# Attention beside a 2-D Fourier filter on one core: the order of the memory terms, and the place of the transposition of the maxima

## The chip, the core and the metric

The kernel runs on one core of one Trainium2 chip. Its time is the device time of one execution in microseconds, as the median of the runs. The engines are named as in the profile: PE (TensorE, with PEld for its weight loads), DVE (VectorE), ACT (ScalarE), POOL (GpSimd) and SP (SyncE, which here only issues transfers).

## What is computed

Two independent heads share one output. The second, a Fourier transform of a 2048 x 576 array, a multiplication and the way back, is not touched by the change. The first is attention with a compressive memory, with 32 heads of 18 columns, over 2048 rows in 4 segments of 512:

```python
for s in range(N):                                  # 4 segments, in order
    logits = einsum("bhqd,bhkd->bhqk", qs, ks) * scale + mask
    a_dot  = einsum("bhqk,bhkd->bhqd", softmax(logits), vs)
    pq  = phi(qs)                                   # phi(t) = t+1 if t>0 else exp(t)
    num = einsum("bhld,bhde->bhle", pq, M)
    den = einsum("bhld,bhd->bhl", pq, z)[..., None] + 1e-6
    outs.append(g * (num / den) + (1 - g) * a_dot)  # g = sigmoid(beta), per head
    M = M + einsum("bhld,bhle->bhde", phi(ks), vs)
    z = z + einsum("bhld->bhd", phi(ks))
```

The rows of all segments are then multiplied by `wo`.

## The kernel before

**Stages.** The program is written out in full by Python, each engine gets its instructions in the order in which the code emits them, and semaphores are set where one engine's instruction needs another's. The forward transform, the projections and the inverse transform fill the time until about 360 us; `ATT.attention` (line 894) does the rest.

**Steps.** `attention` runs 133 steps `t`. A step handles one head of one segment, so 32 steps make a segment, and four steps make a group `k` with its heads `hh` = 0 to 3 ("first" to "fourth" head; the third head's step is `hh==2`). Two groups share a stack `n` of queries `Qs` and keys `Ks` that SP loads from DRAM in six pieces of 144 KB each (`stack_dmas`, line 611). Three pipelines are ten steps apart:

- `s1(t+10)` (629): scores of a head ten steps ahead, for their maxima only. TensorE makes three products into PSUM tiles `s1` (three buffers) and VectorE reduces each (L646, and L640 twice), 512, 512 and 256 columns.
- `mpath` (654), once a group: in the second head's step VectorE, ScalarE and POOL gather the 16 maxima of each row and split them into two bf16 parts `mh` (L658 to L662). TensorE transposes `mh` into a tile `mt` (L665), which takes one of the three `s1` buffers. ScalarE copies it to `mts` (L668, one buffer), and POOL issues a transfer of 8 KB that puts it into two rows of `Qs` (L669). The group needs it when its own steps begin, so that the second product subtracts the maximum.
- `s2(t)` (671): scores with the maximum subtracted, in three products (L679, L683 and L684, L688) into three buffers `s2`, and ScalarE's exponentials into `P`. In the fourth head's step the half above the diagonal is set to zero for the whole group by four instructions, on POOL (L692) for groups 0 to 28, on VectorE (L694, a minimum with a table `cap`) for groups 29 and 30.
- `pv` (700): `P` times the values, five steps later.

**Work in the background.** A list `bg` of generators is advanced by `run_bg` (906): one piece in the middle of a step, and a second at the end of every fifth step (the rate is 1.2). When a segment's outputs of the softmax part are in DRAM (`uD`), a lane fetches the row sums, takes reciprocals and loads tiles `ux` (line 788, three buffers; SP issues), and then appends three jobs to `bg`:

- `combine(g-1)` (792), nine pieces, for the five tiles of 126 rows of segment `g-1`. Piece by piece: TensorE spreads the reciprocals into `pb` (L808), VectorE multiplies `ux` by it (L813), POOL adds the memory term `am` (L814); two pieces later ScalarE rounds the sum to `oh` (L803) and POOL takes the remainder `ol` (L804). From step 117 on VectorE does POOL's two. The loads of `ux` tiles 3 and 4 are issued one step after the pieces of tiles 0 and 1, whose buffers they take.
- five `mem1(g,u)` (775), two pieces each, the memory terms of segment `g` for later use: TensorE's product `pn` (L778), ScalarE's copy to `am` (L780), a load of the next segment's `pq` one step later; then `pb` (L784) and VectorE's multiply (L785).
- `den(g+1)` and `oproj(g-1)`, the denominators and the product with `wo` (L829).

All of these products use one PSUM buffer, tag `post`, so each waits until the engine that reads the one before has finished. The jobs run for `g` = 1, 2, 3, from about steps 51, 84 and 115; below these are the first, second and third time.

## Time and profile before

| | us |
|---|---|
| median of 3 runs shown | 738.96 |
| the three runs | 740.35, 734.36, 738.96 |
| the profiled execution, its own time | 736.84 |
| its span on the core | 735.1 |
| TensorE busy in the span | 691.1 |
| VectorE busy | 553.4 |
| ScalarE busy | 457.9 |
| POOL busy | 204.2 |

A row of a timeline gives start and length in us, engine, line, operation, what it writes and reads, and shape; brackets hold the engine's idle time before it and what ended it. Several of a kind in a row are merged (x4). A row of busy time by stretch gives the stretch, its length, and for each engine the busy time and the number of instructions, then the granted clock of TensorE as a share of full speed, the share of time in which the DMA engines were busy, and GB/s. TensorE's products overlap, so a busy TensorE is not TensorE at its peak, and an idle gap is a lower bound of what was lost.

### The profile page before, as it was taken

The numbers are of one execution on the slowest core, as the hardware profiler recorded it, in microseconds if no ns is written. First come the engines' busy times: TensorE is split into PE (matmuls) and PEld (weight loads), VectorE is DVE, ScalarE is ACT, GpSimd is POOL, SyncE is SP. The second block draws the span as 40 slices with busy tenths as digits, with TensorE's granted clock in tenths as the row PEclk, the third lists the DMA queues.
The fourth block names the chain that finished last, engine by engine and source line by source line (L and its number), as shares of the span: only waits on it lengthen the run. The fifth ranks groups of instructions, "written<-read, shape, count | busy, mean of one in ns | idle before, by whom it ended". The sixth has DMA issues, their size and how long they took to land.

```text
span 735.1 us, 14249 instructions
## 1 busy us (share of the span) xinstructions
PE 691.1 (94%) x4879; PEld 496.6 (68%) x4879; DVE 553.4 (75%) x1285; ACT 457.9 (62%) x1012; POOL 204.2 (28%) x405
## 2 busy tenths in 40 slices
PE   4998999999999999999999999999999899998897
PEld 4988779879779788899744444443665345653396
DVE  6999879899799788787688878876567575668333
ACT  3666796585585664444487777776566566568521
POOL 2111000100200112565065335462334832325100
PEclk9999999999999999999999999999999899999999
DMA  9884435655373468899547656777456565431231
GB/s 337 264 267 148 144 116 180 197 173 160 133 236 113 169 206 277 213 219 219 179 99 185 168 149 162 179 177 145 117 142 161 142 156 131 108 115 41 70 123 64
DMA packets 83243, 121.04 MB, mean 165 GB/s; under 512 B 11352, under 2 KB 50630, under 8 KB 83036
## 3 DMA queue, kind: packets, MB, share of 16 engines
q1 hardware_dynamic: 76580, 104.11, 49.9%
q0 software_dynamic: 6592, 16.03, 8.0%
q8 instruction: 38, 0.62, 0.3%
q14 instruction: 33, 0.27, 0.1%
HBM read 81.78 MB, written 38.24 MB: 163 GB/s over the span
## 4 chain that ended last, share of the span: by engine, by line
PE 70%; DMA 13%; DVE 7%; ACT 5%; issue 3%; POOL 1%; SPq 1%; ACTq 0%; DVEq 0%; POOLq 0%
PE pj L459 14%; PE pv L709 8%; PE po L829 7%; PE pjv L459 7%; PE s L636 4%; PE i L307 4%; PE i L296 3%; PE s L644 3%; PE s L679 3%; DMA x<-qkD 2%; DMA Ks<-qkD 2%; DMA Qs<-qkD 2%; PE pn L778 2%; PE po L858 2%; PE s L683 2%
## 5 line engine op out<-in xcount | busy, mean ns | idle before, releaser
L640 DVE CUSTOM_DVE_ANT_0 junk<-s,mask 128x512 bf16<-128x512 f32 (+1 forms) x256 | 141.2, 551 | 62.6 <-PE s L636 59.0
L646 DVE TENSOR_REDUCE mx<-s 128x4 f32<-128x512 f32 x128 | 87.9, 687 | 12.0 <-PE s L645 9.2
L692 POOL TENSOR_SCALAR_AFFINE_SELECT P<-P 128x512 f32<-128x512 f32 x116 | 70.0, 634 | 73.9 <-ACT P L680 66.0
L709 PE MATMUL pv<-P,vs 128*32 128x512 f32 (+3 forms) x1024 | 89.3, 445 | 0.3 <-DVE P L694 0.3
L680 ACT ACTIVATE P<-s 128x512 f32<-128x512 f32 x128 | 76.3, 596 | 17.4 <-PE s L679 15.0
L689 ACT ACTIVATE P<-s 128x256 f32<-128x256 f32 x128 | 49.1, 384 | 50.9 <-PE s L688 50.9
L685 ACT ACTIVATE P<-s 128x512 f32<-128x512 f32 x128 | 76.0, 594 | 0.3 <-PE s L684 0.3
L459 PE MATMUL pj<-x,wqkh 128*128 128x512 f32 x162 | 56.5, 409 | 0.0
L206 DVE TENSOR_TENSOR Z<-t,t 128x290 f32<-128x290 f32 (+1 forms) x96 | 48.4, 553 | 0.1
L206 DVE TENSOR_TENSOR t<-Z 128x580 f32<-128x580 f32 x64 | 46.0, 754 | 0.0
L506 POOL MEMSET vt<- 128x32 f32 x16 | 2.3, 161 | 153.8 <-PE pm L516 128.7
L636 PE MATMUL s<-Ks,Qs 108*128 108x512 bf16 (+1 forms) x128 | 42.2, 330 | 0.1
L142 PE MATMUL f<-ftab,eh 128*128 128x290 f32 (+1 forms) x160 | 31.4, 315 | 10.1 <-DMA ftab<-ftab 10.1
L296 PE MATMUL i<-civ,Y 128*128 128x256 f32 (+1 forms) x288 | 38.5, 285 | 1.5 <-POOL Y L281 0.9
L296 PEld LDWEIGHTS i<-civ,Y 128*128 128x128 f32 (+1 forms) x288 | 35.9, 181 | 2.3 <-POOL Y L281 1.3
L709 PEld LDWEIGHTS pv<-P,vs 128*32 128x32 f32 x1024 | 22.4, 109 | 21.9 <-issue 14.6
L645 PE MATMUL s<-tri,idb 128*128 128x256 bf16 x128 | 35.2, 275 | 1.3 <-ACT idb L585 1.3
L307 PE MATMUL i<-itab,T 128*128 128x290 f32 (+1 forms) x224 | 36.0, 309 | 0.0
L459 PE MATMUL pj<-xh,wqkl 128*128 128x512 f32 x90 | 35.5, 395 | 0.0
L459 PE MATMUL pj<-x,wqkl 128*128 128x512 f32 x90 | 35.5, 395 | 0.0
L459 PE MATMUL pj<-xh,wqkh 128*128 128x512 f32 x90 | 35.5, 395 | 0.0
L459 PEld LDWEIGHTS pj<-x,wqkh 128*128 128x128 f32 x162 | 30.4, 188 | 7.2 <-issue 0.6
(211 smaller groups left out, 1830.5 us busy)
## 6 DMA issues: line engine op xcount, KB each, us to landing
qkD<-sp SPq DMA_DIRECT2D x36, 384.0 KB
Ks<-qkD SPq DMA_DIRECT2D x72, 144.0 KB
x<-qkD SPq DMA_DIRECT2D x60, 144.0 KB
Qs<-qkD SPq DMA_DIRECT2D x60, 144.0 KB
xin<-xb SPq DMA_DIRECT2D x16, 384.0 KB
cfw<-cfw POOLq DMA_DIRECT2D x16, 384.0 KB, 4.9
civ<-civ POOLq DMA_DIRECT2D x16, 384.0 KB, 7.6
vs<-vD SPq DMA_DIRECT2D x16, 330.0 KB
```

What stands on the lines that cost most here:

```text
L206: v.tensor_tensor(o,a,b,op=op)
L296: nc.tensor.matmul(p[:m,k],Y[i][:,q,c*128:c*128+m],cc[:,hl,o:o+256],start=n==0,stop=n==5)
L307: nc.tensor.matmul(p,x,t,start=n==0,stop=n==6)
L459: s.nc.tensor.matmul(out,a,b,start=i==0,stop=i==len(L)-1)
L636: nc.tensor.matmul(out,Q[:108,h,128*i:128*i+128],K[:108,h,:128*(i+1)],start=True,stop=True)
L640: nc.vector.tensor_tensor_reduce(out=junk[:,:w],in0=src,in1=s.mask[:,512-w:],scale=1.0,scalar=-3.0e38, op0=OP.add,op1=OP.max,accum_out=s.m ...
L646: nc.vector.tensor_reduce(out=s.mx[k][:,hh],in_=pa.rearrange("p (b c) -> p b c",c=128),axis=mybir.AxisListType.X,op=OP.max)
L680: nc.scalar.activation(P[0][:,hh],p0,AF.Exp,scale=SC)
L685: nc.scalar.activation(P[1][:,hh],p1,AF.Exp,scale=SC)
L692: if k<29: nc.gpsimd.affine_select(out=x,in_=x,pattern=pat+[[1,128]],compare_op=OP.is_ge,fill=0.0,base=0,channel_multiplier=-1)
L709: nc.tensor.matmul(s.pvt[32*hh:32*hh+32,128*j:],vt[:,j,19*h:19*h+32],mv[0][:,hh,mv[1]],start=j==0,stop=j==2,skip_group_check=True)
L829: nc.tensor.matmul(ps,a[t][:r,c],b[:r,t,w],start=i==0,stop=i==14)
```

## The change

A new generator `mixed` takes the place of `combine` and the five `mem1` in `bg`. It has the same 19 pieces in another order: five pieces of `combine` first, then memory pieces (`m`) and pieces of `combine` (`c`) in turn. `mpath`'s transposition, which stood in the fourth head's step ahead of the last product of `s2`, moves to the end of the third head's step, and the copy and the transfer's issue move to the beginning of the fourth head's step.

```diff
+    def mixed(s,g):
+        c=s.combine(g-1); M=[s.mem1(g,u) for u in range(5)]
+        for x in "cccccm"+"cmmcmmcmmcmm"+"m":
+            if x=="c": next(c,None); yield
+            else:
+                while M:
+                    try: next(M[0]); break
+                    except StopIteration: M.pop(0)
+                yield
+        for _ in c: pass
+        for m in M:
+            for _ in m: yield
...
-                    bg.append(s.combine(g-1))
-                    for u in range(5 if g<4 else 0): bg.append(s.mem1(g,u))
+                    bg.append(s.mixed(g))
...
             if qu: qu.pop(0)()
+            if hh==3 and m is not None: steps(m,1)
             steps(a,1)
...
             steps(a,1)
-            if hh==3 and m is not None: steps(m,1)
             steps(b,1)
-            if hh==3 and m is not None: steps(m,1)
+            if hh==2 and m is not None: steps(m,1)
```

POOL's queue at a group early in attention (group 2; `P_4719` to `P_4721` are its exponentials, `wol` a piece of the late set-up):

```order
+L669 DMA Qs_3320<-mts 2x16x128
 L608 TENSOR_TENSOR wol<-ob,woh 126x576
 L692 AFFINE_SELECT P_4719<-P_4719 128x4x128
 L692 AFFINE_SELECT P_4720<-P_4720 128x4x128 x2
 L692 AFFINE_SELECT P_4721<-P_4721 128x4x128
-L669 DMA Qs_3320<-mts 2x16x128
```

The issue of the transfer of the maxima now stands ahead of the group's four zero settings, and here of a piece of the set-up too.

VectorE's queue the second time, at steps 86 and 87 (`L813` multiplies tile 3 of `ux`, the `L640` and `L646` rows are reductions of `s1` scores):

```order
+L640 ISA junk,mg<-s_7797,mask 128x256
+L640 ISA mg 128x1
+L646 TENSOR_REDUCE mx<-s_7811 128x4
+L640 ISA junk,mg<-s_7819,mask 128x512
+L640 ISA mg 128x1
 L813 TENSOR_TENSOR ux<-ux,pb 126x512
-L640 ISA junk,mg<-s_7801,mask 128x256
```

The multiply of tile 3 stands one step's reductions later than before; a memory product has taken its place in step 86.

VectorE's queue the third time, at steps 119 and 120 (the first two rows are the multiply and the sum of tile 3, the `L694` rows the four minima of group 29, `L785` the multiply of memory tile 0, and the rows behind it the work on tile 4):

```order
 L813 TENSOR_TENSOR ux<-ux,pb 126x512
 L814 TENSOR_TENSOR am<-ux,am 126x512
+L694 TENSOR_TENSOR P_9064<-P_9064,cap 128x4x128
+L694 TENSOR_TENSOR P_9065<-P_9065,cap 128x4x128 x2
+L694 TENSOR_TENSOR P_9066<-P_9066,cap 128x4x128
+L785 TENSOR_TENSOR am<-am,pb 126x512
 L804 TENSOR_TENSOR ol<-am,oh 126x512
 L813 TENSOR_TENSOR ux<-ux,pb 72x512
 L814 TENSOR_TENSOR am<-ux,am 72x512
```

The minima now stand right behind tile 3 and ahead of the first memory multiply. TensorE's queue in the changed step 120, from its second product of `s2` on (`pb` and `pn` both go into the `post` buffer):

```order
L684 MATMUL s_9196<-x_2763,Ks_3323 128x128
L784 LDWEIGHTS sel
L784 MATMUL pb<-rd,sel 126x512
L688 LDWEIGHTS Ks_3323
L688 MATMUL s_9203<-x_2763,Ks_3323 128x256
L778 MATMUL pn<-pq,Mst_64 126x512
```

Memory tile 0's second product and memory tile 1's first now stand in one step; before, step 120 had neither.

## The prediction

> **What bounds the kernel now.** I read the page's engine table first, then its clock row, then busy time by stretch, and last every pause of TensorE in time order, each with its releaser.

> ```profile
> span 735.1 us, 14249 instructions
> PE 691.1 (94%) x4879; PEld 496.6 (68%) x4879; DVE 553.4 (75%) x1285; ACT 457.9 (62%) x1012; POOL 204.2 (28%) x405
> ...
> PEclk9999999999999999999999999999999899999999
> ```

> TensorE is busy for 94% of the span and the clock is full but for one slice. The change touches the attention stage alone, from about 360 us. There TensorE's program is the path and its pauses are what can be won. Where the clock falls is seen by stretch:

> ```profile
> 573.00:579.60 6.60, 3.46 (x31) 1.65 (x30) 3.24 (x10) 4.18 (x10) 5.00 (x5) 0.98 0.76 198
> 579.60:586.20 6.60, 6.50 (x25) 2.39 (x25) 4.12 (x14) 2.88 (x7) 6.56 (x9) 0.50 0.48 108
> 668.00:692.50 24.50, 20.05 (x146) 7.48 (x142) 14.55 (x25) 18.52 (x43) 4.93 (x8) 1.00 0.23 71
> ```

> The columns are length, busy time of PE, PEld, DVE, ACT and POOL, granted clock, DMA share, GB/s. In the first stretch TensorE stood for 6.60 − 3.46 = 3.14 us, and in the next it ran at half clock: 6.50 × 0.5 = 3.25 us lost. The third is the end of attention's steps, with 24.50 − 20.05 = 4.45 us of idle.

> The pauses that the change can touch are these (start, length, instruction, and in brackets the idle time before it and what ended it):

> ```profile
> 384.87 0.39 PE L679 MATMUL s<-Qs,Ks 110*128 110x512 bf16 x1 [0.43 <-DMA Qs<-mts]
> ...
> 394.44 0.39 PE L679 MATMUL s<-Qs,Ks 110*128 110x512 bf16 x1 [1.49 <-DMA Qs<-mts]
> ...
> 406.47 0.38 PE L644 MATMUL s<-x,Qs 108*128 108x384 bf16 x2 [0.52 <-DMA Ks<-qkD]
> ...
> 453.72 0.38 PE L644 MATMUL s<-Ks,x 108*128 108x384 bf16 x2 [0.27 <-DVE mg L640]
> 455.70 0.38 PE L644 MATMUL s<-Ks,x 108*128 108x384 bf16 x2 [0.61 <-DVE mx L646]
> ...
> 476.52 0.38 PE L644 MATMUL s<-x,Qs 108*128 108x384 bf16 x2 [1.22 <-DMA Ks<-qkD]
> ...
> 481.92 0.38 PE L644 MATMUL s<-x,Qs 108*128 108x384 bf16 x2 [0.28 <-DVE mg L640]
> 483.76 0.38 PE L644 MATMUL s<-x,Qs 108*128 108x384 bf16 x2 [0.22 <-DVE mx L646]
> ...
> 495.02 1.12 PE L778 MATMUL pn<-pq,Mst 126*126 126x512 f32 x2 [0.89 <-DVE am L785]
> ...
> 569.86 0.38 PE L808 MATMUL pb<-rr,sel 96*126 96x512 bf16 x1 [0.55 <-DVE ux L813]
> ...
> 575.47 0.38 PE L808 MATMUL pb<-rr,sel 96*72 96x512 bf16 x1 [1.10 <-DVE ux L813]
> 576.42 0.22 PE L665 MATMUL mt<-idb,mh 128*128 128x128 bf16 x1 [0.33 <-DVE mx L646]
> 577.03 0.38 PE L644 MATMUL s<-x 108*128 108x384 bf16 x2 [0.28 <-DVE mg L640]
> 579.68 0.37 PE L636 MATMUL s<-x 108*128 108x256 bf16 x1 [1.51 <-DVE mg L640]
> ...
> 589.07 0.38 PE L784 MATMUL pb<-rd,sel 96*126 96x512 bf16 x1 [0.51 <-ACT am L780]
> ...
> 603.44 0.38 PE L784 MATMUL pb<-rd,sel 96*126 96x512 bf16 x1 [0.45 <-ACT am L780]
> ```

> **Part 1: the transfer of the maxima.** POOL issues it today behind the four zero settings, and TensorE's first product of the next group but one needs it:

> ```profile
> 385.61 2.40 POOL L692 TENSOR_SCALAR_AFFINE_SELECT P<-P 128x512 f32<-128x512 f32 x4
> 387.95 0.61 POOL L669 DMA_DIRECT2D Qs<-mts  x1
> ...
> DMA to landing us min/median/max: 2.0/5.0/7.6
> ...
> 384.90 0.25 ACT L668 COPY mts<-mt 32x128 bf16<-32x128 bf16 x1 [0.37 <-DMA Qs<-mts]
> ```

> In the changed order the transposition comes one step (about 2.1 us) sooner and the issue no longer waits 2.40 us for the zeros, so the issue moves up by about 3 us. The two waits on it, 0.43 + 1.49 = 1.92 us, are then covered. But right behind them TensorE waits for loads of the stacks (0.52 us at 406.47), and SyncE issues those at the pace at which earlier loads land:

> ```profile
> 394.00:406.00 12.00, 11.51 (x92) 5.18 (x92) 9.30 (x29) 9.17 (x23) 4.39 (x9) 1.00 0.74 188
> ```

> At a DMA share of 0.74 these loads move up only in part. The bounds are 0 (all of it is waited for again at 406) and −1.92; ScalarE's copy of the maxima (0.37 us of wait, with the copy that SyncE's next store needs behind it) goes earlier too, so I take the middle, −1.0. The selects start one transfer's issue (0.61 us) later; their first reader comes two steps on, so that is nothing, and without this cover 0.61 us a group.

> **Part 2: the transposition in the third head's step.** It now waits for POOL's split of the maxima with one step less between. At the regular pace it fits, and its PSUM tile shifts the rotation of three `s1` tiles. So far the fourth head's tile shortened the lead over VectorE at the start of the next group; that is where 453.72 to 455.70 (0.27 + 0.61, behind a reciprocal) waited. Now it is shortened one step sooner, where the second score product of the step waits for the last reduction of the step before:

> ```profile
> 424.67 0.28 PE L636 MATMUL s<-Ks,Qs 108*128 108x256 bf16 x1
> ...
> 425.46 0.38 PE L636 MATMUL s<-Ks,Qs 108*128 108x512 bf16 x1
> ...
> 424.99 0.42 DVE L640 CUSTOM_DVE_ANT_0 junk<-s,mask 128x256 bf16<-128x256 f32 x1 [0.29 <-PE s L636]
> 425.34 0.08 DVE L640 DVE_READ_ACCUMULATOR2_ANT mg<- 128x1 f32 x1
> ```

> The reduction is over at 425.42 and TensorE comes at 425.46, or 0.06 us later with the transposition ahead of it: it just fits. Price 0, gain −0.8 (bounds 0 and −0.88). TensorE's earlier arrival at 476.52, where loads are waited for again, gives back some of parts 1 and 2: 0 to +1.8, taken as +0.5.

> **Part 3: memory terms between the tiles, first time (steps 51 to 65).** The pauses at 481.92, 483.76 and 495.02 go: 0.28 + 0.22 + 0.89 = −1.4. New: step 55 holds a combination tile and a memory multiply, with one `post` bank between them, priced by the like pause at 569.86, 0.55, and step 58 a multiply ahead of the tight reduction, 0.4. Sum −0.5, bounds −1.4 and +0.5. With the memory steps the loads of the next third's `pq` move too: on SyncE's queue one passes ahead of four stack pieces here and one ahead of two in part 4. Among TensorE's pauses none waits for a stack from 484 to 604 us, so this costs 0; uncovered it would be one load's place in that queue.

> **Part 4: the second time (steps 84 to 97).** Here VectorE multiplied tiles 3 and 4 before they had been loaded:

> ```profile
> 574.73 0.69 DVE L813 TENSOR_TENSOR ux<-ux,pb 126x512 f32<-126x512 f32 x1 [2.56 <-DMA ux<-uD]
> ...
> 578.60 0.68 DVE L813 TENSOR_TENSOR ux<-ux,pb 72x512 f32<-72x512 f32 x1 [1.63 <-DMA ux<-uD]
> ...
> 568.95 0.32 SPq L791 DMA_DIRECT2D ux<-uD  x1
> ```

> The load of tile 3 landed about 5.7 us after its issue (568.95 to 574.7), and nothing moves it. The multiply of tile 3 moves one step on, past a product `pn` of 1.1 us, to about 575.0, against 574.7 for the landing; that of tile 4 moves four steps on. So 1.10 + 0.33 + 0.28 + 1.51 goes, and with it the drop of the clock, 3.25; 0.51 and 0.45 go as well, and one pause of 0.5 is new in step 90. Sum: −6.9, bounds −7.4 and 0 (rival 3).

> **Part 5: the third time (steps 115 to 127).** Here the change costs. From step 117 on VectorE does this work instead of POOL, and the zeros of the last groups too:

> ```profile
> 670.31 0.68 DVE L813 TENSOR_TENSOR ux<-ux,pb 126x512 f32<-126x512 f32 x1
> 671.02 0.69 DVE L814 TENSOR_TENSOR am<-ux,am 126x512 f32<-126x512 f32 x1
> ...
> 673.55 2.49 DVE L694 TENSOR_TENSOR P<-P,cap 128x512 f32<-128x512 f32 x4
> ...
> 669.77 0.66 POOL L661 CAST mh<-mg 128x16 bf16<-128x16 f32 x1
> 670.52 0.22 POOL L662 TENSOR_TENSOR mh<-mg,mh 128x16 bf16<-128x16 f32 x1
> ...
> 671.04 0.38 PE L808 MATMUL pb<-rr,sel 96*72 96x512 bf16 x1 [0.96 <-DVE ux L813]
> ```

> In before's clock: the transposition of the last maxima, now in step 118, waits for POOL, 670.74 less the 0.61 of the transfer that has gone ahead: to 670.1, a pause of 0.7. ScalarE then finishes two exponentials and the cast at about 672.3; VectorE does subtraction, multiply and sum of tile 3 until 674.2, the four minima (2.49) until 676.7, and only then the multiply of memory tile 0, until 677.4. Step 120's two products both need the one `post` bank: `pb` waits for the first multiply (1.25 us, to 673.65), `pn` for the last (673.9 to 677.4, 3.45 us). Later ones of 0.5 and 0.7 make 6.6 us of pauses against 4.45: +2.1; followed step by step I get +0.9, since ScalarE has caught up meanwhile. I take +1.5, bounds 0 and +2.1. With 4.7 us of standing in 5.05 us, denser than the 3.14 of 6.60 at 573 us, I expect the clock to drop here as it did there: +3.25, bounds 0 and 3.25.

> [...]

> **Sum**: −1.0 − 0.8 + 0.5 − 0.5 − 6.9 + 1.5 + 3.25 = −3.95 us. The profiled execution took 736.84 us (span 735.1 and 1.7 around it), which gives 732.9; it lies 2.1 us under the median of the runs shown, 738.96, and the runs spread over 6 us. Against the median: 735.0.

> **Rivals.** (1) The clock holds at step 120, because the pause is shorter or cut up differently: −3.95 − 3.25 = −7.2, 731.8 us. For it speaks that ScalarE and VectorE may run ahead; against it that the pause is longer than the one that did drop it. (2) Slower: the tight reduction of part 2 does not fit. A pause of s in each of 31 groups costs 31 s; it decides from s = 0.13 us, and at 0.4 us it is +12.4 − 3.95 = +8.4, 747.4 us. Against it: the margin is measured, if 0.04 us, and the same margin held at the place that the change frees. (3) The load of tile 3 lands later than 575, VectorE's queue stands at step 87 and the clock drops there as before: part 4 is nothing, +2.95, 741.9 us. For it: the margin is 0.3 us. Against it: tile 4, the longer pause, has margin. (4) The change doesn't speed up the transfers' stage, since the stacks' loads bind: parts 1 and 2 nothing, 736.3 us; within the forecast's range.

> **How the numbers follow.** Chances: forecast (with 4) 0.52, rival 1 0.22, rival 2 0.10, rival 3 0.12, others 0.04. Likeliest 735.0 us, alone 731.5 to 738.5. The range 729.5 to 742.0 takes in rival 1 with the runs' spread and rival 3, and leaves out rival 2 and little else. 1% is 7.4 us, about what a measurement of this kernel tells from no change: faster than 731.6 takes rival 1 at its better half and a tail of the forecast, 0.2; slower than 746.4 is rival 2 and a tail of rival 3, 0.11; within, 0.69.

> **What would show it.** Right: no wait on `mts` in TensorE's rows; the granted clock 1.00 through 570 to 590; no VectorE wait on `ux` in part 4; a pause before `pn` (L778) in step 120 of about 3.4 us with VectorE's minima ahead of its multiply, and half clock for some 6 us behind it. Wrong: pauses of TensorE's score product L636 behind VectorE's reductions in every third and fourth head (rival 2), or a wait on `ux` at step 87 (rival 3). A longer wait at 406 or 476 would show parts 1 and 2 given back.

## The result and the profile after

The changed kernel takes 734.62 us (median of 17 runs, 730.96 to 738.64), the kernel before 736.53 us in as many runs beside it (734.25 to 740.35). The ratio, with its 95% interval in brackets, is 0.9962 [0.9946, 0.9977] (the two medians alone give 0.9974): 0.4% faster, 1.7 to 4.0 us, on the quick side of "within 1%". The forecast of 735.0 us is met to 0.4 us, partly by luck: it set −3.95 us against a median of three runs, 738.96, that lies 2.4 us above the median of 17.

The profiled execution took 735.37 us. The first lines of its page:

```profile
span 733.7 us, 14245 instructions
...
PE 691.2 (94%) x4879; PEld 497.7 (68%) x4879; DVE 552.7 (75%) x1285; ACT 457.4 (62%) x1012; POOL 204.6 (28%) x405
...
PEclk9999999999999999999999999999999999998999
```

The slice with the low clock has moved: it lay at 580 us before, it lies at 670 us now. The busy times are nearly those of before, so what changed is waits and the clock. The starts of a step's product at L679 show where the time went. For the last steps, first before, then after (the first row is the start of step 118, the last that of step 127):

```profile
667.01 0.38 PE L679 MATMUL s<-Qs,Ks 110*128 110x512 bf16 x1
...
688.81 0.38 PE L679 MATMUL s<-x,Ks 110*128 110x512 bf16 x1
```

```profile
660.52 0.38 PE L679 MATMUL s<-Qs,Ks 110*128 110x512 bf16 x1
...
687.02 0.38 PE L679 MATMUL s<-x,Ks 110*128 110x512 bf16 x1
```

These steps took 21.80 us and take 26.50: +4.70. The same subtraction for each stretch of steps, of this kernel and of those of the experiments below, in us against before:

| kernel | 0 to 51 | 51 to 65 | 84 to 97 | 118 to 127 |
|---|---|---|---|---|
| the change | −0.03 | −2.30 | −6.61 | +4.70 |
| transposition and transfer alone | +0.70 | −1.03 | −1.36 | +0.85 |
| mixture alone | −1.17 | −1.35 | −6.59 | +4.83 |
| third time in the old order | +1.16 | −2.45 | −6.61 | +0.85 |
| filler in step 120 | −2.60 | −1.54 | −6.58 | +3.10 |
| group 29's zeros on POOL | +0.42 | −2.49 | −6.61 | +4.19 |
| loads of `pq` early | −3.58 | −1.35 | −6.61 | +4.25 |
| third time old, `pq` early | −3.70 | −2.63 | −6.60 | +2.44 |
| mixture in the first two times alone | −0.73 | −1.50 | −6.60 | +2.69 |
| before, `pq` early | +0.81 | +1.44 | −0.85 | +0.01 |
| without group 29's zeros | −2.31 | −2.76 | −6.59 | +1.86 |

What lies between the columns moves by 0.8 us at most. Of the change itself the columns sum to −4.2 us; it started attention 2.42 us later than before did (363.04 against 360.62), with the same program up to there. Part of that, 1.7 us at most (half of its length, an estimate), is a clock drop of 3.4 us at 292.64, at a granted clock of 0.50 and ahead of attention: the six profiled executions with such a drop (the change and numbers 1, 2, 5, 6 and 9) start attention 1.57 to 3.22 us later than before's, the five others from 1.26 us sooner to 0.99 later. So much differs from one execution to the next, and a column is to be believed where several kernels repeat it: that for 84 to 97 does (−6.58 to −6.61 in nine kernels). The first does not as a whole; the account of part 1 below takes it apart.

TensorE's pauses after (start, length, instruction; in brackets the idle time before it and what ended it), those that answer to the rows of the prediction:

```profile
408.27 0.38 PE L644 MATMUL s<-x,Qs 108*128 108x384 bf16 x2 [1.79 <-DMA Ks<-qkD]
...
458.11 0.38 PE L644 MATMUL s<-Ks,x 108*128 108x384 bf16 x2 [1.03 <-DVE mx L646]
...
478.13 0.38 PE L644 MATMUL s<-x,Qs 108*128 108x384 bf16 x2 [0.75 <-DMA Ks<-qkD]
484.31 0.38 PE L784 MATMUL pb<-rd,sel 96*126 96x512 bf16 x1 [0.56 <-DVE am L811]
...
578.89 1.07 PE L709 MATMUL pv<-P,vs 128*32 128x512 f32 x8 [0.38 <-POOL P L692]
584.12 0.38 PE L784 MATMUL pb<-rd,sel 96*126 96x512 bf16 x1 [0.49 <-DVE ux L813]
...
663.42 0.23 PE L665 MATMUL mt<-idb,mh 128*128 128x128 bf16 x1 [0.36 <-POOL mh L662]
666.96 0.38 PE L784 MATMUL pb<-rd,sel 96*126 96x512 bf16 x1 [1.18 <-DVE ux L813]
670.69 2.07 PE L778 MATMUL pn<-pq,Mst 126*126 126x512 f32 x2 [3.24 <-DVE am L785]
680.64 0.27 PE L688 MATMUL s<-x,Ks 110*128 110x256 bf16 x1 [0.42 <-ACT P L689]
681.62 0.38 PE L679 MATMUL s<-x,Ks 110*128 110x512 bf16 x1 [0.71 <-ACT P L680]
684.63 1.12 PE L778 MATMUL pn<-pq,Mst 126*126 126x512 f32 x2 [0.67 <-DVE am L785]
689.72 1.08 PE L778 MATMUL pn<-pq,Mst 72*72 72x512 f32 x2 [0.67 <-DVE am L785]
```

Four things are to be seen. No row between 380 and 400 us waits on `mts` any more, but the wait for the stacks has grown from 0.52 to 1.79 us (below it is the wait at step 21: it stands between the starts of steps 21 and 22 at L679, and the product that waits is the first of step 22). The pauses around 576 us (1.10, 0.33, 0.28, 1.51) are gone. Step 55 has its new pause of 0.56. And step 120 holds 1.18 and 3.24 us. The clock, by stretch:

```profile
405.28:408.69 3.41, 1.62 (x14) 0.49 (x7) 1.51 (x6) 1.17 (x4) 0.41 (x2) 1.00 0.66 171
408.69:412.11 3.42, 3.42 (x17) 1.05 (x16) 1.72 (x4) 1.31 (x3) 0.00 (x0) 0.50 0.64 142
...
564.00:580.00 16.00, 14.94 (x122) 6.93 (x120) 13.91 (x39) 11.80 (x27) 13.21 (x18) 1.00 0.72 186
...
664.69:668.10 3.41, 1.58 (x11) 0.67 (x7) 2.45 (x4) 2.94 (x7) 0.26 (x1) 1.00 0.03 5
668.10:674.90 6.80, 4.21 (x13) 1.16 (x13) 2.53 (x5) 2.08 (x4) 0.00 (x0) 0.50 0.01 2
```

It holds where it dropped before (564 to 580 and on), and within attention it drops behind the two places where pauses are dense: for 3.4 us at 408.69 and for 6.8 us at 668.10.

VectorE's rows at step 120 show what `pn` waits for:

```profile
665.62 0.69 DVE L804 TENSOR_TENSOR ol<-am,oh 126x512 fp32r<-126x512 f32 x1 [3.99 <-ACT oh L803]
666.23 0.68 DVE L813 TENSOR_TENSOR ux<-ux,pb 126x512 f32<-126x512 f32 x1
666.94 0.69 DVE L814 TENSOR_TENSOR am<-ux,am 126x512 f32<-126x512 f32 x1
667.55 2.49 DVE L694 TENSOR_TENSOR P<-P,cap 128x512 f32<-128x512 f32 x4
669.95 0.68 DVE L785 TENSOR_TENSOR am<-am,pb 126x512 f32<-126x512 f32 x1
```

The first row waits 3.99 us for ScalarE's cast, and VectorE's queue behind it goes row by row: multiply and sum of tile 3, four minima, and only then the multiply of memory tile 0 that frees the bank.

### The profile page after: what moved, and what is told of

Read it like the earlier page. It is cut to its first block, busy times and chain, and to the rows that moved or that the text cites. A ratio compares the mean times of both kernels' runs of the same rounds, so it can differ in the third digit from the quotient of the medians.

```text
span 733.7 us, 14245 instructions
## 1 busy us (share of the span) xinstructions
PE 691.2 (94%) x4879; PEld 497.7 (68%) x4879; DVE 552.7 (75%) x1285; ACT 457.4 (62%) x1012; POOL 204.6 (28%) x405
## 4 chain that ended last, share of the span: by engine, by line
PE 70%; DMA 12%; DVE 8%; ACT 5%; issue 3%; POOL 2%; SPq 0%; DVEq 0%; ACTq 0%; POOLq 0%
PE pj L459 14%; PE pv L709 9%; PE po L842 7%; PE pjv L459 7%; PE s L636 4%; PE s L644 3%; PE s L679 3%; DMA yb<-yout 3%; PE i L307 2%; PE i L296 2%; PE pn L778 2%; PE s L683 2%; PE po L871 2%; DMA x<-qkD 2%; PE f L142 2%
## 5 line engine op out<-in xcount | busy, mean ns | idle before, releaser
L640 DVE CUSTOM_DVE_ANT_0 junk<-s,mask 128x512 bf16<-128x512 f32 (+1 forms) x256 | 141.2, 551 | 60.0 <-PE s L636 53.9
L646 DVE TENSOR_REDUCE mx<-s 128x4 f32<-128x512 f32 x128 | 87.9, 687 | 11.5 <-PE s L645 8.7
L680 ACT ACTIVATE P<-s 128x512 f32<-128x512 f32 x128 | 77.4, 605 | 15.6 <-PE s L679 11.9
L685 ACT ACTIVATE P<-s 128x512 f32<-128x512 f32 x128 | 77.3, 604 | 0.3 <-PE s L684 0.3
L692 POOL TENSOR_SCALAR_AFFINE_SELECT P<-P 128x512 f32<-128x512 f32 x116 | 69.8, 637 | 6.0 <-ACT P L689 3.2
L636 PE MATMUL s<-Ks,Qs 108*128 108x512 bf16 (+1 forms) x128 | 42.2, 330 | 0.0
```

Of the source, the lines that this page charges most:

```text
L636: nc.tensor.matmul(out,Q[:108,h,128*i:128*i+128],K[:108,h,:128*(i+1)],start=True,stop=True)
L640: nc.vector.tensor_tensor_reduce(out=junk[:,:w],in0=src,in1=s.mask[:,512-w:],scale=1.0,scalar=-3.0e38, op0=OP.add,op1=OP.max,accum_out=s.m ...
L646: nc.vector.tensor_reduce(out=s.mx[k][:,hh],in_=pa.rearrange("p (b c) -> p b c",c=128),axis=mybir.AxisListType.X,op=OP.max)
L680: nc.scalar.activation(P[0][:,hh],p0,AF.Exp,scale=SC)
L685: nc.scalar.activation(P[1][:,hh],p1,AF.Exp,scale=SC)
L692: if k<29: nc.gpsimd.affine_select(out=x,in_=x,pattern=pat+[[1,128]],compare_op=OP.is_ge,fill=0.0,base=0,channel_multiplier=-1)
```

## The experiments

Theory: the gain is the second time's order (pauses and a clock drop gone), the third time's order gives most of it back through VectorE's queue and a clock drop, and the earlier transfers gain nothing since the stacks' loads bind behind them. The rivals stand in each expectation. All ratios are to the kernel before.

**1. The transposition and the transfer alone.** In the loop of before, `combine` and `mem1` stay:

```diff
+            if hh==3 and m is not None: steps(m,1)
             steps(a,1)
...
-            if hh==3 and m is not None: steps(m,1)
             steps(b,1)
-            if hh==3 and m is not None: steps(m,1)
+            if hh==2 and m is not None: steps(m,1)
```

> Before, with the moves of the maxima alone (transposition in the third head's step, transfer ahead of the zeros); the memory terms stay in their old order. The forecast's terms for these two parts sum to -1.0 - 0.8 + 0.5 = -1.3 us against before. From the changed kernel's trace, where the wait for loads of the stacks behind these parts grew from 0.52 to 1.79 us and the waits at the start of the following group stayed, I now expect about 0 (-0.6 to +0.6 by the steps up to 47), and +1.7 more if the clock drops behind the longer wait. The pauses of 1.10, 0.28 and 1.51 us at steps 86 to 90 and the clock drop behind them must be there as in before. Rival: the transfers were the bound of that stretch and the gain is -1.9 us or more, with no longer wait at step 21.

Measured: 0.9983 [0.9956, 1.001], and +0.70 us in the steps to 51. The wait behind the transfers grew further:

```profile
408.14 0.41 PE L644 MATMUL s<-x,Qs 108*128 108x384 bf16 x2 [2.65 <-DMA Ks<-qkD]
...
579.63 0.37 PE L636 MATMUL s<-x 108*128 108x256 bf16 x1 [1.39 <-DVE mg L640]
```

The clock dropped behind the first (408.4 to 411.8) and, as in before, at 579.0 to 585.8; of the 1.10 us before tile 4's product 0.31 stayed. The +0.70 us lies 0.4 us below the least that was expected with a drop. The rival falls, and the second time's gain isn't this part's, but for 1.4 us of its pauses.

**2. The mixture alone**: the change with the three `mpath` lines at their old places.

> The changed kernel with the transposition and the transfer back at their old places: the mixture alone. By the theory that the whole effect is the mixture's, the attention steps end about 3.9 us earlier than in before: -2.3 in the first time (steps 51 to 65), -6.6 in the second (84 to 97), +5.0 in the third (115 to 127); the waits on the transfers of the maxima (0.43 and 1.49 us) and the reciprocal's pauses stand as in before, and the wait for the stacks at step 21 is about 0.5. Rival: the gain at steps 84 to 97 needs the earlier transposition too (the pause behind the reduction of the maxima, 1.51 us, would stay); then -6.6 shrinks to about -3 and the whole is about 0.

Measured: 0.9963 [0.9941, 0.9984], the ratio of the whole change, and columns −1.35, −6.59, +4.83. Of the waits on the maxima 0.25 and 1.47 us stand, and none for the stacks at step 21:

```profile
386.42 0.39 PE L679 MATMUL s<-Qs,Ks 110*128 110x512 bf16 x1 [0.25 <-DMA Qs<-mts]
395.97 0.39 PE L679 MATMUL s<-Qs,Ks 110*128 110x512 bf16 x1 [1.47 <-DMA Qs<-mts]
...
669.67 2.07 PE L778 MATMUL pn<-pq,Mst 126*126 126x512 f32 x2 [3.25 <-DVE am L785]
```

By the medians the mixture is the whole effect; the rival, that the second time needs the transposition too, falls. In the first time the mixture alone is 0.95 us short of the change, but the seven kernels with both range from −1.35 to −2.76, and the load's wait in that stretch from none to 1.51 us, so that a share of the transposition there isn't shown.

**3. The third time in the old order.**

```diff
-                    bg.append(s.mixed(g))
+                    if g<3: bg.append(s.mixed(g))
+                    else:
+                        bg.append(s.combine(g-1))
+                        for u in range(5): bg.append(s.mem1(g,u))
```

> The changed kernel with the third time (steps 115 to 127) in the old order, all tiles of the combination ahead of the memory terms, and the mixture in the first two times. By the theory that the mixture costs about 5 us in the third time (pauses before pb and pn in step 120, and a clock drop behind them), this is 5 us faster than the changed kernel, about -5 / 734.6 = -0.7% (-0.4 to -0.9%), and about -1.0% against before; no pause over 1 us before pn, and full clock through the steps 118 to 127. Rival: what was lost in the third time is lost by the earlier transposition in step 118 and by the order of VectorE's minima, whatever the combination's order; then the time stays within 1.5 us of the changed kernel's.

Measured: 0.9894 [0.9859, 0.9928], 730.8 us: 0.7% under the change, as expected. The last steps cost +0.85 instead of +4.70, at full clock. What is left there is the earlier transposition, waiting for POOL's split of the maxima:

```profile
405.77 0.38 PE L644 MATMUL s<-x,Qs 108*128 108x384 bf16 x2 [3.12 <-DMA Ks<-qkD]
...
661.40 0.23 PE L665 MATMUL mt<-idb,mh 128*128 128x128 bf16 x1 [1.51 <-POOL mh L662]
```

The first row shows the stacks' wait at its worst, with a drop behind it.

**4. Filler in step 120**, to take the clock drop and leave the waits:

```diff
+        def filler(n):
+            f=s.ps1.tile([128,512],F32,name="s1",tag="s1")
+            for i in range(n):
+                nc.tensor.matmul(f.rearrange("p (a c) -> p a c",a=4),s.idb,s.tri[:,None,:].to_broadcast([128,4,128]),start=True,stop=True)
...
+            if t==120: filler(5)
             run_bg(1.2)
...
+            if t==120: filler(13)
             run_bg(0)
```

> The changed kernel with 18 extra products of 128x512 in bf16 on TensorE in step 120, whose result nobody uses: 5 ahead of the combination's product pb and 13 ahead of the memory term's product pn, to fill the two pauses (1.18 and 3.24 us) there. The waits stay, only TensorE isn't idle in them. By the theory that the third time's loss is a stall of some 1.5 to 1.8 us and a clock drop of 6.8 us at half rate (3.3 to 3.4 us lost), the time falls by about 3.3 us against the changed kernel (-1.5 to -3.4, as far as the filler fits into the pauses), and the clock is 1.00 from 660 to 690 us. Rival: the loss is all stall, and the clock's drop costs nothing since TensorE waits for VectorE and ScalarE there anyway; then 0, or up to +0.5 where the filler is longer than the pause.

Measured: 0.9922 [0.9887, 0.9957]. The waits are filled, and the clock is full; `pb` and `pn` still start within 0.06 us of the multiplies that they wait for, so the filler delays neither:

```profile
667.51 1.12 PE L778 MATMUL pn<-pq,Mst 126*126 126x512 f32 x2 [0.44 <-DVE am L785]
```

```profile
664.00:671.00 7.00, 6.56 (x37) 2.54 (x39) 3.67 (x7) 2.79 (x8) 0.00 (x0) 1.00 0.01 2
```

The steps 118 to 127 cost +3.10 instead of +4.70: the drop was worth 1.6 us, the stall 3.1. Both theories miss. The drop isn't free, but of the 6.8 us at half clock in the change only 4.21 had work in them (row further up), which at half rate loses 2.1, as an estimate; and part of that was likely waited for anyway. The median is 0.4% under the change's, but its interval doesn't tell 1.6 from 3.3 us; the −2.60 of the first column, which the filler can't touch, is in it too (the wait at step 21 was 0.95 us there, and no drop came).

**5. Group 29's zeros on POOL**: in `s2`, `if k<29` becomes `if k<30`.

> The changed kernel with the causal zeros of group 29 set by POOL instead of VectorE (group 30 and 31 stay): the four minima (2.49 us) no longer stand between the last tile's work of the combination and the multiply of memory tile 0. By the theory that the pause before pn in step 120 is VectorE's queue, it shrinks from 3.24 us to below 1, the clock holds through 668 to 675, and the time is 4 to 5 us less than the changed kernel's (ratio to before about 0.990). Rival: the pause hangs on ScalarE's subtractions, which must be over before that multiply; then pn still waits about 3 us, on ScalarE or on VectorE's earlier multiplies, and the time stays within 1 us of the changed kernel's.

Measured: 0.9935 [0.991, 0.9959], and +4.19 in the last steps. The pause before `pn` shrank as the theory said, and the one before `pb` grew; first TensorE, then VectorE and POOL:

```profile
668.34 0.58 PE L784 MATMUL pb<-rd,sel 96*126 96x512 bf16 x1 [2.76 <-DVE ux L813]
669.77 2.08 PE L778 MATMUL pn<-pq,Mst 126*126 126x512 f32 x2 [0.64 <-DVE am L785]
```

```profile
656.35 0.68 DVE L813 TENSOR_TENSOR ux<-ux,pb 126x512 f32<-126x512 f32 x1
...
665.40 2.29 DVE L804 TENSOR_TENSOR ol<-am,oh 126x512 fp32r<-126x512 f32 x1 [3.99 <-POOL P L692]
```

```profile
655.38 1.81 POOL L692 TENSOR_SCALAR_AFFINE_SELECT P<-P 128x512 f32<-128x512 f32 x3
...
664.74 2.39 POOL L692 TENSOR_SCALAR_AFFINE_SELECT P<-P 128x512 f32<-128x512 f32 x4
```

The subtraction (L804) took 2.29 us instead of 0.69, beside POOL's selections. Its row names POOL as what ended the wait of 3.99 us, but ScalarE's cast of the same tile had ended 0.11 us before it began, as in the change:

```profile
664.69 0.60 ACT L803 CAST oh<-am 126x512 fp32r<-126x512 f32 x1
```

3.40 us of pauses remain of 4.42, and the clock dropped as in the change. Neither theory had this; number 10 leaves the selections out.

**6. The loads of `pq` early.**

```diff
-            if 16<=t<21: s.pq_load(1,t-16)
+            if t<5: s.pq_load(1,t)
```

> The changed kernel with segment 1's five loads of pq issued at steps 0 to 4 instead of 16 to 20, where they stand among the stacks' loads. By the theory that the loads of the stacks swallow the gain of the earlier transfer, the wait at step 21 (1.79 us) and the clock drop behind it go: 2 to 3 us less than the changed kernel's profiled run, about -0.3% in the medians (the drop came in that run and in the run with the transposition alone and not in the one with the mixture alone). Rival: the wait there is on the landing of the piece just issued, whose issue hangs on the ring of its buffers and not on the queue's load; then it stays at 1 to 2 us, and the clock drops as often.

Measured: 0.9904 [0.9876, 0.9933], 0.6% under the change. The stretch from 380 to 412 us, first the change, then this kernel:

```profile
380.00:412.00 32.00, 29.95 (x242) 13.21 (x240) 24.92 (x80) 23.81 (x58) 15.65 (x28) 0.95 0.72 172
```

```profile
380.00:412.00 32.00, 31.75 (x277) 14.94 (x275) 27.67 (x88) 26.56 (x65) 18.25 (x33) 1.00 0.68 169
```

2.05 us of idle became 0.25 and the clock holds; the steps to 51 are 3.6 us shorter than before's. On SyncE's queue the six loads of `Qs`, which the waiting product reads, are now issued one behind the other from 394.69 us, where the last two of the change were issued from 399.34 on, behind three loads of `pq`; first the change, then this kernel:

```profile
399.34 1.18 SPq L620 DMA_DIRECT2D Qs<-qkD  x2
```

```profile
394.69 3.26 SPq L620 DMA_DIRECT2D Qs<-qkD  x6
```

The rival falls: the stacks were late because other loads stood among theirs.

**7. Third time old, `pq` early**: both edits.

> Third time in the old order and segment 1's loads of pq at steps 0 to 4, both in one kernel: the mixture in the first two times, the earlier transposition and transfer as in the changed kernel. If the two theories hold, their gains add: the third time's order was worth 0.7% against the changed kernel, the loads 0.3%, so about 0.986 of before. Rival: the loads gain nothing; then it stands where the kernel with the third time in the old order alone stood, 0.989.

Measured: 727.56 us, 0.9871 [0.9838, 0.9903], the lowest ratio here. The first three columns are near those of numbers 6 and 3: −3.70, −2.63, −6.60. The last, +2.44, holds a drop at 663.8 that number 3 had not, behind pauses of 0.70 us for ScalarE and 0.52 for VectorE that number 3 has too (0.71 and 0.52). The interval overlaps with that of number 3, so that the two gains' adding up is shown by the trace, in these columns, and not by the medians.

**8. The mixture in the first two times alone**: before, with the edit of number 3 and `mixed`.

> Before, with the mixture in the first two times alone; the third time and the moves of the maxima stay as they were. By the theory that the first two times gain about 2 and 6.6 us and that the moves of the maxima are worth nothing, it stands where the kernel with all but the third time's mixture stood: 0.989 of before (0.986 to 0.992), with the waits of 0.43 and 1.49 us on the maxima back and the wait at step 21 near 0.5 us. Rival: the earlier transposition is worth 1 to 2 us in the medians, hidden in the changed kernel's profile by a clock drop at step 21 that most runs don't have; then it is at 0.991 to 0.992.

Measured: 0.9916 [0.9888, 0.9945]. This lies at the border of the two expectations, 0.2% above number 3 with overlapping intervals: inconclusive on what the earlier transposition is worth in the medians. The waits on the maxima (0.31 and 1.37 us) and at step 21 (0.33) are there as expected. Its third time has the order of before to the instruction, and yet cost +2.69, because the clock dropped at 665.7 behind pauses (0.97 and 0.84 us) that before has too (0.96 and 0.84).

**9. Before, with `pq` early** and nothing else.

> Before, with segment 1's five loads of pq at steps 0 to 4 instead of 16 to 20 and nothing else. If the moves of the maxima and the earlier loads only gain together (the transfers' wait and the loads' wait stand one behind the other), this is worth no more than before's own wait at step 21, 0.52 us: ratio 0.999 (0.996 to 1.001), and the waits of 0.43 and 1.49 us on the maxima stay. Rival: the loads' place alone is worth the 3 us that it was worth in the changed kernel; then 0.996.

Measured: 0.9978 [0.9954, 1.0002], half way between the two expectations, with both inside the interval; the waits on the maxima stay:

```profile
388.15 0.39 PE L679 MATMUL s<-Qs,Ks 110*128 110x512 bf16 x1 [0.48 <-DMA Qs<-mts]
397.92 0.39 PE L679 MATMUL s<-Qs,Ks 110*128 110x512 bf16 x1 [1.69 <-DMA Qs<-mts]
```

The wait at step 21 is gone and the steps to 51 took 0.81 us more than before's, with a clock drop of 3.4 us behind the 1.69, which is up to 1.7 (half of 3.4). Without that drop they would be up to 0.9 us shorter than before's, as an estimate. The profiled execution was also the slowest of the twelve (741.62 us), with a second drop at 481.2 behind a wait of 1.87 us for the stacks. So what the loads alone gain stays open, between nothing and the rival's 3 us.

**10. Without group 29's zeros**, on any engine: `if k==29: return` at the head of `sel`. That group's masked entries are left as they are. All lines from there on have a number one higher.

> The changed kernel with the causal zeros of group 29 left out on every engine (that group's masked entries stay as they are), so that neither VectorE's four minima nor a POOL selection beside VectorE stands at step 119. Theory: POOL's selections stretched VectorE's subtraction from 0.69 to 2.29 us when the zeros were given to POOL, and so moved the pause from pn to pb; without either, pb waits about 1.2 us as in the changed kernel and pn about 0.6, the pauses of step 120 are 1.8 instead of 4.4 us, and the step is 2.5 us shorter at least (more where the clock holds): 0.4 to 0.9% under the changed kernel, ratio to before 0.987 to 0.992. Rival: with POOL, the selections were waited for (VectorE's row named POOL's selection as what ended its wait) and ScalarE's subtraction binds; then the pause before pb is still over 2 us.

Measured: 0.9895 [0.9865, 0.9925], 0.7% under the change. TensorE, then VectorE:

```profile
662.08 0.38 PE L785 MATMUL pb<-rd,sel 96*126 96x512 bf16 x1 [1.18 <-DVE ux L814]
663.41 1.36 PE L779 MATMUL pn<-pq,Mst 126*126 126x512 f32 x2 [0.84 <-DVE am L786]
```

```profile
660.74 0.69 DVE L805 TENSOR_TENSOR ol<-am,oh 126x512 fp32r<-126x512 f32 x1 [3.99 <-ACT oh L804]
```

Pauses of 2.02 instead of 4.42 us, and +1.86 in the last steps instead of +4.70; a clock drop of 3.4 us at 664.16 is still in it. The subtraction again comes after 3.99 us, of ScalarE, and takes 0.69. So the 3.99 us of number 5 were not a wait for POOL, as its row has it; beside POOL's selections the subtraction itself took 2.29 us, and without them 0.69. The minima are 2.4 of the 3.24 us; the 1.18 us before `pb` stand, behind ScalarE.

## Why the prediction came out right

By its steps, in us:

| step | forecast | change's profile | what the runs showed |
|---|---|---|---|
| parts 1 and 2 | −1.3 | −0.03 | with late `pq`: −2.3 and −2.6 without a clock drop, −0.03 to +1.2 with one; with early `pq`: −3.6 and −3.7 |
| part 3 | −0.5 | −2.30 | −1.35 for the mixture alone, −1.35 to −2.76 with the moves of the maxima |
| part 4 | −6.9 | −6.61 | repeated in nine kernels |
| part 5, stall | +1.5 | +4.70 with the next | +3.1 with the clock held |
| part 5, clock | +3.25 | | +1.6 |

**Right, and shown.** Part 4: the pauses between steps 84 and 97 fell from 4.73 to 1.73 us, which with the drop of 3.25 makes 6.25 of 6.61. Tile 3's load landed in time, so rival 3 didn't come: its multiply started 0.09 us behind the end of its product `pb` (575.53), and its row names no load.

```profile
575.62 0.69 DVE L813 TENSOR_TENSOR ux<-ux,pb 126x512 f32<-126x512 f32 x1 [0.56 <-issue]
```

The mechanism of part 5 held too: 1.18 and 3.24 us for `pb` and `pn` against 1.25 and 3.45 forecast, VectorE's minima ahead of the multiply, and a drop behind. Rival 2 (the tight reduction) appears in no trace: no row of L636 waits at each group. Rival 1 needed the clock to hold; where the filler made it hold, it gave 1.6 us and not the 3.25 that set it apart.

**The failed steps.** Part 1: "so I take the middle, −1.0". By the start of step 21, counted from the start of attention, the change was 1.91 us ahead of before, all of the 1.92 of the two waits. Then 1.27 us was waited for again (1.79 instead of 0.52: the loads did "move up only in part", by a third), and 1.6 us went to the clock drop behind that wait, which the forecast had not thought of: at step 23 the change was 1.0 us behind. Steps 23 to 43 brought that 1.0 us back, with no pause that shows how. The loads of `pq` that stood among the stacks' on SyncE's queue were not looked at in the forecast, and number 6 shows that they bound. The outcome is rival 4's, by one cause more than it named.

Most of this repeats. The eight kernels with the moves of the maxima are 1.91 to 2.05 us ahead at step 21, and steps 26 to 43 take 35.60 to 35.61 us in each, against 36.38 in before. What differs between them is the wait at step 21 and the clock. In numbers 4 and 10 it was 0.95 and 1.20 us and no drop followed; in the change and in numbers 1, 3 and 5 it was 1.79 to 3.12 us, with a drop. So by step 51 the kernels with the moves stood 2.3 us and more ahead of before or not at all, by that wait and its drop, where the forecast took a middle value (with late `pq` and without the moves, before and numbers 8 and 2 stand at 0, −0.73 and −1.17). The early loads of `pq` gain 1.0 to 1.4 us beside an execution without the drop, and 3.6 us or more beside one with it.

Part 2: "gain −0.8". The pauses of 0.27 and 0.61 us came back as one of 1.03 at 458.11 us, at the start of the same group. All eight kernels with the move have the one pause of 1.03, and the others the two. So moving the transposition's tile one step sooner didn't give the lead back. In the change's trace VectorE works off two reciprocals of 0.95 us among the reductions ahead of that pause (from 453.97 and 456.56 us), as in before; that they use up the lead is likely, and no run left them out.

Part 3: "step 58 a multiply ahead of the tight reduction, 0.4" didn't come, and part of the load's wait (1.22 to 0.75) and a pause of 0.30 at 470.42 went beyond the pauses that were forecast to go. By the columns the misses of parts 1 and 2 (+1.3) and of part 3 (−1.8) nearly cancel too, which was luck.

Part 5 was right in its sum, +4.7 against +4.75, by two errors that cancel. The stall was mis-sized at "+1.5, bounds 0 and +2.1": the pauses of the last steps are 7.25 us (the seven rows from 663.42 on: 0.36 + 1.18 + 3.24 + 0.42 + 0.71 + 0.67 + 0.67; the last lies just behind the start of step 127) against 4.01 before, +3.2. The 6.6 us of the forecast were near; the step "ScalarE has caught up meanwhile" wasn't true: two pauses of 0.42 and 0.71 behind ScalarE and two of 0.67 behind VectorE remained. And the clock's drop was priced as if TensorE had work all the time at half rate (3.25), while it stood for 2.59 of the 6.80 us.

## What to carry to other kernels

When a wait goes, find the next one in the same stretch and what stands on the queue ahead of the late transfer: here moving five loads that nobody needed yet saved 3.6 us where the edit's gain had been swallowed by a wait and a clock drop, and about 1 us where no drop had come; what it saves by itself stayed open. One order of work can be right twice and wrong the third time, when another engine has taken over a piece (VectorE the zeros): look at each use of a loop by itself. A clock drop isn't to be priced at half of its length: here one of 6.80 us, at half clock, had 4.21 us of work in it and cost 1.6 us, where half of the work is 2.1 and half of the length 3.4.

## What the runs showed of the hardware

```profile
391.62:395.03 3.41, 1.92 (x25) 0.90 (x17) 1.91 (x8) 1.54 (x6) 2.81 (x6) 1.00 0.92 234
...
575.95:579.37 3.42, 1.61 (x10) 0.79 (x9) 1.79 (x5) 2.58 (x6) 2.04 (x3) 1.00 0.76 183
579.37:582.78 3.41, 3.08 (x13) 1.25 (x16) 3.15 (x10) 1.36 (x3) 3.41 (x5) 0.50 0.62 142
```

1.49 us idle in the first, and the clock held; 1.81 in the second, and it fell. In the traces of before and of the change, of the windows of the grid at full clock from 360 to 690 us, the three with 1.79 us of idle or more (1.81 in before, 1.79 and 1.84 in the change) were followed by half clock, and every other one, with 1.49 or less, by full clock. But the change's drop at 292.64 followed a window with 1.42 us, less than the 1.49 at which the clock held in before. Pauses of the same length went with a drop or with none by where they fell on the grid: in number 8, 0.97 and 0.84 us fell into one window (662.25 to 665.66, 1.85 us idle in all), and in before into two (0.96 and 1.25 us idle in all). This is likely part of the 4 to 11 us that runs of one kernel differ by; that it is most of it wasn't tried.

**A VectorE subtraction took 2.29 us beside POOL's selections.** That is L804 at 665.40 in number 5, with the selections from 664.74 to 667.13; without them it took 0.69, in the change and in number 10. The multiply L813 at 656.35 in number 5 took 0.68 beside selections that ran from 655.38 to 657.19. That is one instance of each, and why the one took longer and the other didn't wasn't shown. The subtraction ended 0.56 us behind the last selection (667.69 against 667.13), so it may have stood until POOL was done rather than run slowly; its row doesn't tell. The profile put the idle time before it down to POOL, and ScalarE's cast, 0.11 us before it began, shows that it wasn't POOL's.
